# Attention and a gated feed-forward layer on one core: weight rows and weight columns regrouped by four, beta loaded in place

## The chip, the cores and the metric

The kernel runs on one core of a Trainium2 chip. The core has five engines that run side by side and wait for one another by semaphores: PE (TensorE, matrix products), DVE (VectorE), ACT (ScalarE), POOL (GpSimd) and SP (SyncE, which here only issues transfers). PEld is the weight loading of PE, a row of its own in the profile. Transfers (DMA) are issued by SP, ACT or POOL and carried by 16 DMA engines. The metric is the device time of one execution in microseconds (us); lower is better.

## The reference

The reference computes causal attention for 4 batches of 8 heads, 768 positions and 64 values a head, and sends the result through a feed-forward layer. Heads 0, 2 and 6 see all earlier positions; the others see the first 4 positions and a window of 64.

```python
scores = q @ k.T / sqrt(64)                 # per batch and head, masked as above
a      = softmax(scores)
x      = (a @ v) laid out as [3072 tokens, 512]
h      = x @ w_in                           # [3072, 2048]
g      = h * (1 / (1 + exp(-beta * h)))     # beta has one value for each of the 2048 columns of h
out    = g @ w_out                          # [3072, 512]
```

The columns of h, the values of beta and the rows of w_out share one index, d_ff (0 to 2047). The sum in the last line runs over it, so that it may be walked in any order, if it is the same order for all three.

## The kernel before

The work is cut into 8 chunks (4 batches, 2 halves of 384 positions) and 32 units (a chunk and a pair of heads). A unit is loaded, transposed, multiplied to scores (`sp`, lines L422 and L451, PE), sent through the exponential (`es`, L460, ACT), masked (L478 and following, DVE) and multiplied with the values (`po`, L520, PE), normalized on DVE and transposed to `xT`. A chunk of `xT` then passes the feed-forward layer in two parts:

- Part one (`steps_G1`) goes by 16 groups `fi` of 128 columns of h. A group has 4 products over d_model (L588, each with a weight load of 128x128 from `w_in_sb` and 384 tokens passing), a tanh on ACT with beta as scale (`th`, L593), and a gate on DVE (`gT`, L596).
- Part two (`steps_G2`) sums over the 16 groups for 128 tokens at a time: 16 products (L641, L626 for the last tokens) with `gT` as weights and `w_out_sb[:, fi, :]` passing; ACT copies the sum out (`osb`) and SP stores it.

Both weight matrices stay in SBUF in bf16. Each is loaded by 4 POOL transfers, which also convert from float32: `load_w_in` (L140) takes a quarter of w_in's columns (512 of them, all four blocks of 128 rows); `load_w_out` (L144) takes 512 rows of w_out. Beta is loaded at the start by ACT as 16 rows of 128, transposed by PE (`beta_go`, L671) and halved on DVE into `beta_h` (L672).

The order of the instructions on each engine is written out by hand and kept: `RAMP` is a list of words for the first 8 units, `PLAN` and `TAIL` for the rest. In `RAMP`, `lq` and `lv` are loads of q, k and v on SP; `wi0` to `wi3` and `wo0` to `wo3` the weight loads on POOL; `ck`, `cq`, `cv` casts; `tk`, `tq` transposes on PE and `kk`, `kq` their copies; `ma` masks on DVE; `be` beta; `hm` and `hf` the first and the second half of a group of part one, `mm` and `mA` a whole group, `mb` a piece of part two. Every engine works its list strictly in order. What an instruction waits for (semaphores of other engines and of transfers) is derived from the tiles that it reads and writes. The transfers of SP and ACT share 8 semaphores in turn, so that each of them waits for the one issued 8 before it; POOL's transfers have 8 of their own (`DMASW0` to `DMASW7`), and the weight loads are the first eight of these.

Of the kernel before, what the change touches and what calls it, by code (L numbers as in the profile page):

```python
# [10 lines left out]
F32 = mybir.dt.float32  # L11
BF16 = mybir.dt.bfloat16
ALU = mybir.AluOpType
# [5 lines left out]
def kernel(  # L19
# [13 lines left out]
    nc = tc.nc  # L33
# [4 lines left out]
    FO = d_ff // 128  # L38
    HALF = S // 2
# [16 lines left out]
    stage = ctx.enter_context(tc.tile_pool(name="stage", bufs=2))  # L56
# [5 lines left out]
    ps_m = ctx.enter_context(tc.tile_pool(name="ps_m", bufs=3, space=bass.MemoryType.PSUM))  # L62
# [10 lines left out]
    def later(delay, fn):  # L73

        todo = [fn]

        def once():
            if todo:
                todo.pop()()
        heapq.heappush(heap, (clock[0] + delay, count[0], once))  # L80
        count[0] += 1
        return once

    def flush(upto):
        while heap and heap[0][0] <= upto:
            heapq.heappop(heap)[2]()

    def step(s):
        cost, fn = s
        flush(clock[0])  # L90
        clock[0] += cost
        fn()
# [4 lines left out]
    xT = {}  # L97
# [36 lines left out]
    w_in_sb = wpool.tile([128, MO, d_ff], BF16, name="w_in_sb")  # L134
    w_out_sb = wpool.tile([128, FO, d_model], BF16, name="w_out_sb")
    beta_h = wpool.tile([128, FO], F32, name="beta_h")
# [4 lines left out]

    def load_w_out(i):
        f = slice(i * 4, (i + 1) * 4)
        nc.gpsimd.dma_start(out=w_out_sb[:, f, :], in_=moe_w_out.rearrange("(fo fi) d -> fi fo d", fi=128)[:, f, :])  # L144
        w_done.add(i)

    load_qk(0, 0, 2)
# [1 line left out]
    warm = consts.tile([1, 1], F32, name="warm")  # L149
    nc.vector.memset(warm, 0.0)  # L150
    nc.scalar.activation(out=warm, in_=warm, func=ACTF.Exp)
    br = stage.tile([FO, 128], F32, name="beta_r", bufs=1)
    nc.scalar.dma_start(out=br, in_=moe_beta.rearrange("(fo fi) -> fo fi", fi=128))


    zeros = consts.tile([128, 512], BF16, name="zeros")
# [1 line left out]
    ident_f = consts.tile([128, 128], F32, name="idf")  # L158
# [81 lines left out]
    def cast(u, name, copy):  # L240
        b, h2, p = units[u]
        c = u // NPAIR
        s = st_u.setdefault(u, {})
        if "qkb" not in s:
            s["qkb"] = att.tile([128, 2, HT, 2, D], BF16, name="qkb", bufs=4)
        copy(out=s["qkb"][:, "qk".index(name)], in_=staged[name, c, p // 2][:, p % 2:4:2].rearrange("p h t d -> p t h d"))
# [328 lines left out]
    def spare_bank():  # L575
        return ps_s.tile([128, 2, 512], F32, name="sp")[:, 0]
# [3 lines left out]
    def steps_G1(c):  # L580
        def begin(fi):
            if c not in gTs:
                gTs[c] = moe.tile([128, FO, HALF], BF16, name="gT")
            return spare_bank() if wide[0] else ps_m.tile([128, 512], F32, name="mm")

        def product(fi, hp, some):
            for mo in some:
                nc.tensor.matmul(hp[:, 0:HALF], w_in_sb[:, mo, fi * 128:(fi + 1) * 128], xT[c][:, mo, :],  # L588
                                 start=(mo == 0), stop=(mo == MO - 1))

        def end(fi, hp):
            th = moe.tile([128, HALF], F32, name="th", bufs=3)
            nc.scalar.activation(out=th, in_=hp[:, 0:HALF], func=ACTF.Tanh, scale=beta_h[:, fi:fi + 1])  # L593

            def gate():
                nc.vector.scalar_tensor_tensor(out=gTs[c][:, fi, :], in0=th, scalar=1.0, in1=hp[:, 0:HALF],  # L596
                                               op0=ALU.add, op1=ALU.mult)
            gates.setdefault(c, []).append(later(700, gate))

        def grp(fi, some=range(MO)):  # L600

            def go():
                if 0 in some:
                    partial[c, fi] = begin(fi)
                product(fi, partial[c, fi], some)
                if MO - 1 in some:
                    end(fi, partial.pop((c, fi)))
            return (len(some) * 163, go)
        halves[c] = lambda fi, i: grp(fi, range(i * MO // 2, (i + 1) * MO // 2))
        return [grp(fi) for fi in range(FO)]  # L610
# [55 lines left out]
    due = [max(i for i, x in enumerate(first) if x[0] == c) + 1 for c in range(NCHUNK)]  # L666
    done = [0, 0]

    def beta_go():
        bp = ps_m.tile([128, 512], F32, name="mm")  # L670
        nc.tensor.transpose(bp[:, 0:FO], br, ident_f[0:FO, 0:FO])  # L671
        nc.vector.tensor_scalar(out=beta_h, in0=bp[:, 0:FO], scalar1=0.5, scalar2=None, op0=ALU.mult)  # L672

    def run(steps):
        for x in steps:
            step(x)
# [8 lines left out]
    def do(word):  # L685

        what, n, i, eng = re.fullmatch(r"([a-z]{2}|[a-z][A-Z])(\d*)\.?(\d*)([vag]?)", word).groups()
        n, i = int(n or 0), int(i or 0)
        if what in ("ck", "cq"):
            cast(n, what[1], copies[eng])  # L690
        elif what in ("tk", "tq"):
            step((170, lambda: transpose_qk(n, what[1])))
        elif what in ("kk", "kq"):
            copy_qk(n, what[1], copies[eng])
        elif what == "ko":
            sinks_of(n)
        elif what in ("ad", "qk", "ex", "ma"):
            if n not in visits:
                visits[n] = steps_QK(n)
            step((0 if what in ("ex", "ma") else 170, lambda: visits[n][what](i)))  # L700
        elif what == "cv":
            cast_v(n, i, copies[eng])
        elif what == "vo":
            sink_values(n)
        elif what == "pv":
            pv = products.setdefault(n, [])
            if not pv:
                pv.extend(steps_PV(n))
            run(pv[:2])
            del pv[:2]  # L710
        elif what == "no":
            normalize(n)
        elif what == "xd":
            x_by_dma(n)
        elif what == "xx":
            run(steps_X(n))
        elif what == "cx":
            copy_x(n, copies[eng])
        elif what == "on":
            ones_v(engines[eng], n)  # L720
        elif what == "ne":
            negatives([(0, 1, 2), (3, 4)][n])
        elif what == "be":
            step((100, beta_go))
        elif what == "lv":
            load_v(n, held=eng == "g", tiles=[i])
        elif what == "lq":
            load_qk(n, i, held=eng == "g")
        elif what == "wi":
            load_w_in(n)  # L730
        elif what == "wo":
            load_w_out(n)
        elif what == "rq":
            rows_queries()
        elif what == "rk":
            rows_keys()
        elif what == "ro":
            if n not in more_rows:
                more_rows[n] = load_rows(n)
            more_rows[n].pop(0)()  # L740
        elif what in ("dk", "dq"):
            transposes_dma(n, what[1])
        elif what == "ml":
            late[n].pop(0)()
        elif what == "tt":
            run(steps_T(n))
        elif what == "hm":
            opened.append(done[0])
            done[0] += 1
            step(halves[0](opened[-1], 0))  # L750
        elif what == "hf":
            step(halves[0](opened.pop(0), 1))
        else:
            feed({"mm": "a", "mA": "A", "mb": "b"}[what])

    def feed(x):
# [12 lines left out]
            wide[0] = False  # L769

    RAMP = """
        on0g ck0a lv0.0g cq0g lv0.1 ne0 ck2a tq0 ck1v cq1g lv0.2 lq1.0g kq0a be tk0 ne1 kk0v tq1
        ad0.0 qk0.0 ad0.1 kq1a tk2 lq1.1g qk0.1 lv1.0 ex0.0 cv0.0g ck3v cv0.1v lv1.1 ad1.0 cq2a cq3g ex0.1 tk1
        tk3 ad1.1 kk1a kk2a pv0 kk3a tq2 ko1 ko2 vo0 qk1.1 qk1.0 cv0.2g kq2a ex1.1 ck4v pv0 wi0
        lv1.2 ad2.0 ex1.0 ad2.1 qk2.0 qk2.1 tq3 pv1 lq2.0 pv0 pv1 pv1 cq4g lv2.0 tq4 ko3 ex2.0 ad3.0
        kq3a ml0 ex2.1 tk4 pv2 no0 qk3.0 ad3.1 ck5g qk3.1 no1 kk4a xx0 ex3.0 ck6v tk6 pv3 cq5g
        kq4v pv2 pv3 ad4.0 pv2 ex3.1 ck7g ad4.1 ad5.0 qk4.1 cq6g lv2.1 no2 cq7g lv2.2 kk6a pv3 cx0a
        tq5 ko6 kq5v tk5 ex4.1 qk4.0 kk5a ad5.1 ko5 tq6 qk5.0 no3 wi1 tq7 tk7 ex4.0 qk5.1 xx1
        ad6.0 kq6v ex5.0 wi2 qk6.0 kk7v wi3 on1v ex5.1 ad6.1 lq2.1g qk6.1 ma5.0 cv1.0g ml1 ko7 rk cv1.1g
        cx1a ex6.0 hm ma5.1 cv1.2g ex6.1 mm lv3.0g mA kq7v vo1 pv4 wo0 hf pv4 lv3.1 ad7.0 pv4  # L780
        wo1 lv3.2 pv5 no4 qk7.0 wo2 ex7.0 ad7.1 wo3 pv5 qk7.1 rq pv5 pv6 hm cq8g no5 pv7
        pv6 ex7.1 pv7 pv7 ml1 hf pv6 xx2 no7 no6 cx2a mA mA xx3 cx3a mm mm mm
        mA ro3 mm mm mm mA ck8a mA mm mm mm ro3 mA ro3 mm mm mA mA
        mm ro3 ro3 mm mm mA mA mm mm mA tt8 mA mb ro3 mb mb mb mb
    """
    words = RAMP.split()
    on_vector = {int(w[2]) for w in words if w.startswith("ma")}
# [33 lines left out]
    for t in range(8, NU + 2):  # L821
        c, i = (t + 5) // NPAIR, (t + 5) % NPAIR
# [3 lines left out]
        c, i = (t + 4) // NPAIR, (t + 4) % NPAIR  # L826
        if t >= 12 and c < NCHUNK and i < HT:
            later(2500, lambda c=c, i=i: load_v(c, tiles=[i]))
        c, i = (t + 3) // NPAIR, (t + 3) % NPAIR
# [30 lines left out]
    i = 0  # L860
# [39 lines left out]
```

## Time and profile before

| | before |
|---|---|
| median of 3 runs (lowest to highest) | 229.83 us (229.36 to 231.32) |
| the profiled execution: time, span | 230.81 us, 228.8 us |
| PE, PEld busy in the span | 218.9 us, 125.3 us |
| ACT, DVE, POOL busy | 156.6, 139.3, 87.7 us |
| part one on PE (L588): 512 products of 384 tokens | 326 ns each in the record |
| part two on PE (L641): 368 products of 512 columns | 379 ns each in the record |
| w_in loads (L140): 4 of 512 KB, issue to landing | 9.3 us median |
| w_out loads (L144): 4 of 512 KB, issue to landing | 16.4 us median |
| beta load: 8 KB, issue to landing | 4.1 us |

The times in the views are microseconds from the start of the span. A matmul's record includes its way through the array, and the next one starts before it ends; how fast PE works shows in the distance of their starts. A line of a view by time names start, length, engine, source line, operation and operands; "x6" says that six instructions were merged, and a bracket at the end gives the idle time of that engine just before and what ended it. In the views a transfer stands with the engine that issues it.

### The profile page before, as it was taken

To read this page: it belongs to the slowest core of one execution; us is meant where nothing else is said; L and a number is where in the kernel's file an instruction comes from. 1 tells how busy PE (TensorE), PEld (TensorE's weight loads), DVE (VectorE), ACT (ScalarE), POOL (GpSimd) and SP (SyncE) were. 2 spreads that over 40 slices of the span, in tenths; PEclk is the share of its full clock that TensorE was granted. 3 is DMA by queue.
4 is the path that set the end of the run, shared out by engine and by line. 5 is a ranking of instruction groups with operands and counts; after the bars stand their busy time and mean duration, and the time that the engine had idled before them with its cause. 6 is when DMAs were issued, how large, how long until landed. Compare 5 with 4: busy or idle time off the path is not lost.

```text
span 228.8 us, 5022 instructions
## 1 busy us (share of the span) xinstructions
PE 218.9 (96%) x1907; PEld 125.3 (55%) x1907; DVE 139.3 (61%) x333; ACT 156.6 (68%) x261; POOL 87.7 (38%) x147
## 2 busy tenths in 40 slices
PE   6679999999999999899999999999999999999993
PEld 2446765554655665546654565456645566456553
DVE  3357788853584879327951697576895488128600
ACT  3869899947767797637962796788866687138521
POOL 6386952158360449920296005980180000000000
PEclk9999999999999999999999999999999999999999
DMA  6999999999999499999699668899673111110012
GB/s 205 233 303 230 229 199 197 197 220 170 171 185 190 95 134 156 141 197 165 162 96 140 159 115 126 123 177 108 132 86 83 47 57 27 49 56 36 0 50 92
DMA packets 95384, 31.67 MB, mean 138 GB/s; under 512 B 81776, under 2 KB 92416, under 8 KB 95360
## 3 DMA queue, kind: packets, MB, share of 16 engines
q1 hardware_dynamic: 58880, 22.82, 50.3%
q0 software_dynamic: 35904, 8.13, 41.6%
q10 hardware_dynamic: 576, 0.40, 0.6%
q8 instruction: 15, 0.25, 0.5%
q14 instruction: 9, 0.07, 0.1%
HBM read 27.27 MB, written 6.29 MB: 147 GB/s over the span
## 4 chain that ended last, share of the span: by engine, by line
PE 89%; DMA 6%; SPq 2%; issue 0%; DVE 0%; ACTq 0%; POOL 0%; ACT 0%; DVEq 0%; POOLq 0%
PE mm L641 34%; PE mm L588 25%; PE sp L588 12%; PE sp L451 6%; PE po L520 6%; DMA s<-in_q_dram 4%; DMA QTD<-s 2%; PE mm L626 2%; PE mm L322 1%; SPq L132 1%; PE sp L422 1%; PE mm L558 1%; PE mm L451 1%; PE mm L520 1%; SPq L119 0%
## 5 line engine op out<-in xcount | busy, mean ns | idle before, releaser
L641 PE MATMUL mm<-w_out_sb,gT 128*128 128x512 bf16 x368 | 86.4, 379 | 0.0
L460 ACT ACTIVATE es<-sp 128x768 bf16<-128x768 f32 (+2 forms) x72 | 56.7, 844 | 14.3 <-PE sp L451 14.2
L588 PEld LDWEIGHTS <-w_in_sb 128*128 128x128 bf16 x512 | 47.6, 98 | 29.5 <-issue 0.2
L588 PE MATMUL mm<-xT,w_in_sb 128*128 128x384 bf16 x344 | 63.6, 326 | 0.0
L593 ACT ACTIVATE th<-mm,beta_h 128x384 f32<-128x384 f32 x86 | 49.0, 589 | 6.6 <-PE mm L588 2.3
L596 DVE SCALAR_TENSOR_TENSOR gT<-th,mm 128x384 bf16<-128x384 f32 x86 | 46.2, 552 | 9.6 <-ACT th L593 5.9
L641 PEld LDWEIGHTS <-gT 128*128 128x128 bf16 x368 | 33.0, 98 | 34.4 <-issue 0.9
L282 POOL DMA_DIRECT2D s<-in_q_dram x30 | 22.4, 771 | 43.1 <-DMA QTD<-s 37.5
L645 ACT ACTIVATE osb<-mm 128x512 f32<-128x512 f32 x23 | 13.8, 601 | 32.1 <-PE mm L641 31.2
L588 PE MATMUL sp<-xT,w_in_sb 128*128 128x384 bf16 x168 | 33.0, 326 | 0.0
L520 PEld LDWEIGHTS <-es 128*128 128x128 bf16 x472 | 24.1, 98 | 13.9 <-issue 1.7
L520 PE MATMUL po<-VX,es 128*128 128x65 bf16 x360 | 26.6, 194 | 0.5 <-POOL VX L251 0.5
L593 ACT ACTIVATE th<-sp,beta_h 128x384 f32<-128x384 f32 x42 | 24.4, 585 | 3.1 <-PE sp L588 0.7
L596 DVE SCALAR_TENSOR_TENSOR gT<-th,sp 128x384 bf16<-128x384 f32 x42 | 22.9, 552 | 5.1 <-ACT th L593 3.2
L282 POOL DMA_DIRECT2D s<-in_k_dram x30 | 22.3, 754 | 8.1 <-DMA w_out_sb<-in_moe_w_out_dram 5.2
L478 DVE TENSOR_TENSOR es<-es,Mh 128x768 bf16<-128x768 bf16 (+1 forms) x26 | 17.0, 679 | 13.1 <-ACT es L460 12.5
L451 PE MATMUL sp<-QTD,KT 64*128 64x128 bf16 (+2 forms) x258 | 18.9, 240 | 0.8 <-DMA QTD<-s 0.6
L251 POOL CAST VX<-vs 128x512 bf16<-128x512 f32 x17 | 10.9, 649 | 20.0 <-DMA vs<-in_v_dram 20.0
L529 DVE RECIPROCAL rec<-po 128x6 f32<-128x6 f32 x28 | 5.3, 191 | 18.8 <-PE po L520 18.8
L533 DVE TENSOR_TENSOR x<-po,rec 128x384 bf16<-128x384 f32 x28 | 15.6, 558 | 1.0
L451 PEld LDWEIGHTS <-KT 64*128 64x128 bf16 x278 | 11.2, 94 | 6.9 <-issue 5.1
L259 POOL COPY VO<-VX 128x512 bf16<-128x512 bf16 x16 | 9.6, 622 | 5.1 <-DVE VX L251 5.1
(71 smaller groups left out, 156.4 us busy)
## 6 DMA issues: line engine op xcount, KB each, us to landing
vs<-in_v_dram SPq DMA_DIRECT2D x24, 256.0 KB, 5.8
out_dram<-osb SPq DMA_DIRECT2D x23, 256.0 KB, 2.9
w_in_sb<-in_moe_w_in_dram POOLq DMA_DIRECT2D x4, 512.0 KB, 9.3
w_out_sb<-in_moe_w_out_dram POOLq DMA_DIRECT2D x4, 512.0 KB, 16.4
s<-in_k_dram POOLq DMA_DIRECT2D x30, 64.0 KB, 4.5
s<-in_q_dram POOLq DMA_DIRECT2D x30, 64.0 KB, 4.6
s<-in_k_dram SPq DMA_DIRECT2D x4, 384.0 KB, 6.8
s<-in_q_dram SPq DMA_DIRECT2D x4, 384.0 KB, 8.7
```

The lines of the kernel that those rows point to most:

```text
L251: copy(out=VX[b % 2][:, h2 * HT + t, :, 0:D], in_=staged["v", c][:, t])
L282: nc.gpsimd.dma_start(out=ROWS[c % 2, name][:, t, i * 4 * D:(i + 1) * 4 * D].rearrange("p (h d) -> p h d", d=D), in_=src[b, i:H:2, r:r + 1 ...
L451: nc.tensor.matmul(sps[i][r][:, x * 128:y * 128], key(a, lhs), s["QT"][half(a), qi * 128:(qi + y - x) * 128], start=first, stop=first or y ...
L460: nc.scalar.activation(out=views[i].rearrange("p r k j -> p r (k j)"), in_=banks[2][:, :, 0:n * 128], func=ACTF.Exp, scale=scale)
L478: nc.vector.tensor_mul(ev[:, :, 0:n], ev[:, :, 0:n], Mh[h2][:, None, m0:m0 + n].to_broadcast([128, 2, n, 128]))
L520: nc.tensor.matmul(po[:, qi, hh, :], e, val, start=(j == 0), stop=(j == len(lst) - 1))
L533: nc.vector.tensor_mul(xg[g][:, :, :, u % 2, :].rearrange("p a t d -> p t a d"), po[:, :, :, 0:D], rec.to_broadcast([128, HT, 2, D]))
L588: nc.tensor.matmul(hp[:, 0:HALF], w_in_sb[:, mo, fi * 128:(fi + 1) * 128], xT[c][:, mo, :], start=(mo == 0), stop=(mo == MO - 1))
L593: nc.scalar.activation(out=th, in_=hp[:, 0:HALF], func=ACTF.Tanh, scale=beta_h[:, fi:fi + 1])
L596: nc.vector.scalar_tensor_tensor(out=gTs[c][:, fi, :], in0=th, scalar=1.0, in1=hp[:, 0:HALF], op0=ALU.add, op1=ALU.mult)
L641: nc.tensor.matmul(op, gTs[c][:, fi, ns * 128:(ns + 1) * 128], w_out_sb[:, fi, :], start=(fi == 0), stop=(fi == FO - 1))
L645: nc.scalar.activation(out=osb, in_=op, func=ACTF.Copy, scale=0.5)
```

## The change

The index d_ff is walked in another order. Before, group `fi` held the columns 128 fi to 128 fi + 127. Now the groups go by four: within a block q of 512, group 4q + f holds the columns 512 q + 4 p + f for p = 0 to 127. With that a partition p needs four rows of w_out that lie next to each other in memory (8 KB in float32), which one descriptor fetches, where four pieces of 2 KB were needed. The products of part one read their weights from `w_in_sb` with a step of four columns; w_in itself is loaded as before. Beta is loaded in that order straight to its 128 partitions, in pieces of four values, so that the transpose falls away; the load moves from ACT, at the start, to SP, behind the v loads of the second chunk (new word `lb`), and the halving on DVE (word `be`) moves to just ahead of the first `hm`. `beta_go` no longer counts as a step of 100 in the planner's clock. Lines after the beta load have numbers one lower than before, up to the new function (L588 becomes L587).

```diff
     def load_w_out(i):
         f = slice(i * 4, (i + 1) * 4)
-        nc.gpsimd.dma_start(out=w_out_sb[:, f, :], in_=moe_w_out.rearrange("(fo fi) d -> fi fo d", fi=128)[:, f, :])
+        nc.gpsimd.dma_start(out=w_out_sb[:, f, :], in_=moe_w_out.rearrange("(q fi f) d -> fi q f d", fi=128, f=4)[:, i])
...
-    br = stage.tile([FO, 128], F32, name="beta_r", bufs=1)
-    nc.scalar.dma_start(out=br, in_=moe_beta.rearrange("(fo fi) -> fo fi", fi=128))
+    br = stage.tile([128, FO], F32, name="beta_r", bufs=1)
...
-                nc.tensor.matmul(hp[:, 0:HALF], w_in_sb[:, mo, fi * 128:(fi + 1) * 128], xT[c][:, mo, :],
+                nc.tensor.matmul(hp[:, 0:HALF], w_in_sb[:, mo, fi // 4 * 512 + fi % 4:(fi // 4 + 1) * 512:4], xT[c][:, mo, :],
                                  start=(mo == 0), stop=(mo == MO - 1))
...
+    def load_beta():
+        nc.sync.dma_start(out=br.rearrange("p (q f) -> p q f", f=4), in_=moe_beta.rearrange("(q fi f) -> fi q f", fi=128, f=4))
+
     def beta_go():
-        bp = ps_m.tile([128, 512], F32, name="mm")
-        nc.tensor.transpose(bp[:, 0:FO], br, ident_f[0:FO, 0:FO])
-        nc.vector.tensor_scalar(out=beta_h, in0=bp[:, 0:FO], scalar1=0.5, scalar2=None, op0=ALU.mult)
+        nc.vector.tensor_scalar(out=beta_h, in0=br, scalar1=0.5, scalar2=None, op0=ALU.mult)
...
         elif what == "be":
-            step((100, beta_go))
+            beta_go()
+        elif what == "lb":
+            load_beta()
```

In the words of `RAMP`:

```diff
-        ... lq1.0g kq0a be tk0 ne1 ...
+        ... lq1.0g kq0a tk0 ne1 ...
-        ... wi0 lv1.2 ad2.0 ...
+        ... wi0 lv1.2 lb ad2.0 ...
-        ... cx1a ex6.0 hm ma5.1 ...
+        ... cx1a ex6.0 be hm ma5.1 ...
```

More of the change, by code (lines that the diff above doesn't have):

```diff
@@ L771 @@
     RAMP = """
[L772 to L775, printed above, removed]
+        on0g ck0a lv0.0g cq0g lv0.1 ne0 ck2a tq0 ck1v cq1g lv0.2 lq1.0g kq0a tk0 ne1 kk0v tq1 ad0.0
+        qk0.0 ad0.1 kq1a tk2 lq1.1g qk0.1 lv1.0 ex0.0 cv0.0g ck3v cv0.1v lv1.1 ad1.0 cq2a cq3g ex0.1 tk1 tk3
+        ad1.1 kk1a kk2a pv0 kk3a tq2 ko1 ko2 vo0 qk1.1 qk1.0 cv0.2g kq2a ex1.1 ck4v pv0 wi0 lv1.2
+        lb ad2.0 ex1.0 ad2.1 qk2.0 qk2.1 tq3 pv1 lq2.0 pv0 pv1 pv1 cq4g lv2.0 tq4 ko3 ex2.0 ad3.0
         kq3a ml0 ex2.1 tk4 pv2 no0 qk3.0 ad3.1 ck5g qk3.1 no1 kk4a xx0 ex3.0 ck6v tk6 pv3 cq5g
@@ L779 @@
         ad6.0 kq6v ex5.0 wi2 qk6.0 kk7v wi3 on1v ex5.1 ad6.1 lq2.1g qk6.1 ma5.0 cv1.0g ml1 ko7 rk cv1.1g
[L780 to L784, printed above, removed]
+        cx1a ex6.0 be hm ma5.1 cv1.2g ex6.1 mm lv3.0g mA kq7v vo1 pv4 wo0 hf pv4 lv3.1 ad7.0
+        pv4 wo1 lv3.2 pv5 no4 qk7.0 wo2 ex7.0 ad7.1 wo3 pv5 qk7.1 rq pv5 pv6 hm cq8g no5
+        pv7 pv6 ex7.1 pv7 pv7 ml1 hf pv6 xx2 no7 no6 cx2a mA mA xx3 cx3a mm mm
+        mm mA ro3 mm mm mm mA ck8a mA mm mm mm ro3 mA ro3 mm mm mA
+        mA mm ro3 ro3 mm mm mA mA mm mm mA tt8 mA mb ro3 mb mb mb
+        mb
     """
```

## The prediction

> **What bounds the kernel now.** I read four views in this order: busy time by engine, the chain that ended last, the order in time of TensorE, and the order in time of GpSimd with the landings of its loads.
>
> ```profile
> PE 218.9 (96%) x1907; PEld 125.3 (55%) x1907; DVE 139.3 (61%) x333; ACT 156.6 (68%) x261; POOL 87.7 (38%) x147
> ...
> PE 89%; DMA 6%; SPq 2%; issue 0%; DVE 0%; ACTq 0%; POOL 0%; ACT 0%; DVEq 0%; POOLq 0%
> ```
>
> TensorE (PE) is busy 96% of the span and holds 89% of the last chain. Where the missing 10 us lie shows in a table by stretches (PE, PEld, DVE, ACT, POOL busy, then clock, DMA share, GB/s):
>
> ```profile
> 23.00:35.30 12.30, 12.30 (x124) 8.19 (x123) 9.70 (x23) 10.93 (x19) 8.68 (x15) 1.00 1.20 213
> 35.30:47.00 11.70, 11.70 (x78) 7.18 (x76) 9.71 (x18) 10.66 (x21) 2.96 (x4) 1.00 1.22 195
> 47.00:60.00 13.00, 13.00 (x90) 6.12 (x89) 6.01 (x16) 8.31 (x16) 8.94 (x12) 1.00 1.61 202
> 60.00:90.00 30.00, 29.96 (x317) 18.22 (x316) 22.22 (x60) 23.54 (x39) 13.60 (x19) 1.00 1.42 149
> 90.00:96.00 6.00, 5.40 (x68) 3.17 (x66) 3.02 (x8) 3.04 (x5) 5.94 (x10) 1.00 1.65 142
> 96.00:150.00 54.00, 53.99 (x445) 29.58 (x444) 32.96 (x85) 36.51 (x61) 23.44 (x35) 1.00 1.00 141
> 150.00:222.00 72.00, 71.98 (x555) 39.99 (x552) 44.01 (x94) 46.05 (x76) 9.65 (x13) 1.00 0.44 70
> ```
>
> From 23 to 222 us PE is idle for 0.66 us in all, 0.60 of it in one place near 95 us. So from 23 us on nothing that another engine or a transfer gets earlier can shorten the kernel, and whatever stops PE is added in full. The order in time around 23 us, PE first, then POOL:
>
> ```profile
> 22.85 1.15 PE L588 MATMUL mm<-xT,w_in_sb 128*128 128x384 bf16 x6
> 23.84 0.81 PE L588 MATMUL sp<-xT,w_in_sb 128*128 128x384 bf16 x4
> ...
> 13.35 0.88 POOL L140 DMA_DIRECT2D w_in_sb<-in_moe_w_in_dram  x1
> 20.50 2.22 POOL L140 DMA_DIRECT2D w_in_sb<-in_moe_w_in_dram  x3
> 35.52 0.74 POOL L282 DMA_DIRECT2D s<-in_k_dram  x1 [1.79 <-DMA w_in_sb<-in_moe_w_in_dram]
> ```
>
> The first product with w_in starts at 22.85. Only the first quarter of w_in is there by then: issued at 13.35, it took 8.4 us to land (21.8). The other three were issued between 20.5 and 22.7, just ahead. The line's own view, for the last one (issued at 22.0):
>
> ```profile
> DMA to landing us min/median/max: 13.3/13.3/13.3
> ```
>
> So the fourth quarter lands at 22.0 + 13.3 = 35.3 us, and a POOL load that waits for the same semaphore starts at 35.52. PE runs through 23 to 35 without a gap because each product waits for its own quarter alone, and the later quarters are wanted later.
>
> **The change part by part.** *The strided weight columns.* The old group fi reads 128 adjacent columns, inside one quarter; the new group reads every fourth column of the same quarter, so the data it needs is the same. What it waits for is not. The instruction lists of the two kernels as built differ here (row, line, instruction, wait), before first:
>
> ```
> 400 L588 Ldweights w_in_sb [waits DMASW0_49]
> 402 L588 Ldweights w_in_sb
> ...
> 399 L587 Ldweights w_in_sb [waits DMASW0_49]
> 401 L587 Ldweights w_in_sb [waits DMASW3_49,DMASW2_49,DMASW1_49]
> ```
>
> DMASW0 to 3 are the four w_in loads. Before, the waits for 1, 2 and 3 stand at rows 554, 662 and 694, hundreds of instructions later; now all three stand at the second weight load of the first group. Step and blocks together seem to be taken as one interval that crosses all four loads. PE works its list in order, so everything behind row 401 waits too: the po products of attention, the scores, ACT's tanh, DVE's gates. PE would issue row 401 at about 23.0 and gets it at 35.3: **12.3 us**. Nothing in the diff moves the three issues at 20.5 to 22.7: POOL's list is the same up to there. Bounds: from the 35.52 on, POOL starts a load each time the next w_out load lands, at 35.52, 38.86, 42.25 and 45.58, so a load takes about 3.35 us; the earliest landing is 20.5 + 7.2 (the shortest issue to landing of the line) + 2 x 3.35 = 34.4. The latest: beta's packets, below, 1.0 us more, 36.3. Stall 11.4 to 13.3 us.
>
> *PE's restart.* The longest PE idle in this trace after the first matmul is 1.0 us, so the price of a 12 us stop has no row. The nearest is the beginning, where PE comes from rest: eight matmuls of 512 columns (L167) from 1.29 take 3.59 us, the last one 0.63 of it, that is (3.59 - 0.63) / 7 = 0.42 us each; in L641 at the end 32 of them take 7.07 us, 0.22 each. The eight cost some 8 x 0.2 = **1.7 us** more than later. I take this once; bounds 0 (no slow stretch) and 3.4 (twice as long). The clock column says 1.00 there too, so I go by the spacing.
> [...]
>
> *The width of the strided loads.* 512 weight loads of L588 (98 ns each in the groups) run beside matmuls that follow each other every 0.65 / 4 = 162 ns (four from 23.84, the next group 0.65 later). What a contiguous load really occupies shows in L520: 26 pairs of weight load and 65-column matmul take 0.95 us, the last record 0.19, so a pair takes 30 ns. A step of 8 bytes could make that four times as long, 120 ns, and is still covered by 162. I take 0; lower bound 0, upper in the rivals.
>
> *w_out by 8 KB rows.* 4 x 512 pieces become 4 x 128. The bytes stay; four POOL instructions of 756 ns get shorter at most. Before, the w_out loads landed from about 38 to 48 us and PE's first product with them was at 47.2; with PE 14 us later this has slack. 0.
>
> *beta.* Gone are an ACT issue (416 ns, while ACT loads its table), a 201 ns matmul that PE waited 0.7 us for (6.16), and a DVE instruction of 175 ns. But the chain up to 14.8 us is a row of SP issues and the landing of a q load (9.55, 5.26 us to landing), on which PE waits again; the 0.7 falls into that. Moving beta also shifts the eight shared semaphores by one, so that SP's loads wait for a transfer one earlier; SP is issuing without a break from 4.75 to 9.4, so that yields nothing. 0, bounds 0 to -0.3.
> Added are one SP issue behind the v loads (about 17 us) with 512 pieces of 16 bytes. The mean packet of that queue took 50.3% x 16 x 228.8 / 58880 = 31 ns, so 512 of them are 1.0 us of all 16 engines at most, by which SP's later loads (L119, L132) slide; their users stand behind row 401. And a DVE instruction that now waits for beta, just ahead of a mask and a QTD copy that ran at 22.6 and 22.9. SP's loads of that time land 7.6 to 10.9 us after issue, so beta lands at 25 to 28 and DVE stands for 2 to 5 us. This is hidden under PE's stop until 35.3; without the stop PE's products behind those masks would wait as long.
>
> *The gap near 95 us.* PE waits 0.60 us there for a QTD transpose. POOL's row loads no longer wait for w_out once PE is 14 us later, so half may go: -0.3, bounds 0 and -0.6.
>
> **Sum.** 12.3 + 1.7 + 0 + 0 + 0 - 0.3 = +13.7 us. The profiled execution took 230.81 (span 228.8 and 2.0 around it), which gives 244.5. It lies 1.0 above the median of the three runs, 229.83; for the median I say **243.5**. Lowest terms: 11.4 + 0 - 0.6 - 0.3 = +10.5, that is 240.3. Highest: 13.3 + 3.4 = +16.7, that is 246.5.
>
> **The rivals.** *The wait does not bite (not slower).* If the three loads had landed before PE came to row 401, or the wait fell away, PE would run on and the change would be worth beta alone: 229.5 to 229.8. It decides at 23.0 us, the landing of the last quarter against that. For it: groups 0 to 3 need nothing of the other quarters. Against it: the built list, and landings of 7.2 to 13.3 us after issues at 20.5 to 22.0. 4%.
> *Strided loads bound PE as well.* From 162 ns on, a load sets the pace of all 512. Were it eight times the contiguous 30 ns, 240 ns, that adds 512 x 78 ns = 40 us: 283. For it: no row has a stepped weight read. Against it: 130 ns are free per load. 6%.
> *Beta lands last.* The v loads around 22 us took 21.6 us to land; at that pace beta would come at 17 + 21.6 = 38.6, DVE would hold the masks, and the stop would end 3.3 us later, 246.8. Against it: beta has 512 short packets and goes ahead of those loads. 5%.
>
> **How the numbers follow.** The forecast has 85%. The range takes in the bounds of landing and restart, and a little for how single runs lie (229.36 to 231.32): 239.5 to 247.5; it leaves out the first two rivals, 10%, and a tail of the forecast. A measurement of this kernel can tell about 1%, 2.3 us, from no change. Faster by more than that has no mechanism here: 1%. Within 1% is the first rival: 4%. Slower: 95%.
>
> **What would show it.** Right: one PE gap of about 12 us from 23 us, ended by the w_in load, at the second weight load of L587; matmul spacing doubled for some 3 to 4 us after it; then no idle; all later stages moved by about 14 us; L587 at 162 ns a matmul. Wrong: PE running through 23 to 35 us, spacing above 162 ns in the products with w_in, or PE waiting for beta_h or masks after the w_in loads have landed.

## The result, and the profile after

| | before | changed |
|---|---|---|
| median of 4 runs (lowest to highest) | 230.57 us (229.36 to 231.56) | 243.41 us (242.98 to 244.76) |
| the profiled execution: time, span | 230.81, 228.8 us | 242.98, 240.9 us |

The changed kernel takes 1.0569 times as long (95% interval 1.0494 to 1.0645). The forecast was 243.5. Ratios, here and below, leave out executions over 1.5% longer than the fastest of the same kernel; medians and ranges hold all of them.

On the page of the changed kernel, PE's share has fallen although it does the same work (the row of busy tenths, one digit for each 6 us, has a hole in its fifth and sixth slice, and the granted clock is low in the fifth to seventh), and one group of products has an idle time before it that names its releaser:

```profile
PE 219.9 (91%) x1887; PEld 133.7 (55%) x1906; DVE 138.2 (57%) x333; ACT 156.6 (65%) x261; POOL 87.9 (36%) x147
...
PE   7786039999999999999999999999999999999993
...
PEclk9999558999999999999999999999999999999999
...
L587 PE MATMUL mm<-xT,w_in_sb 128*128 128x384 bf16 x344 | 64.9, 330 | 11.9 <-DMA w_in_sb<-in_moe_w_in_dram 11.8
L587 PEld LDWEIGHTS <-w_in_sb 128*128 128x128 bf16 x512 | 55.5, 114 | 35.9 <-issue 13.7
```

(PE's count is 20 lower than before; one of them is beta's transpose, and the other 19 are records missing from the trace, since PEld has only one less, beta's.) In order of time on PE, the first product with w_in runs alone, and the second comes 12 us later:

```profile
21.77 0.35 PE L587 MATMUL mm<-xT,w_in_sb 128*128 128x384 bf16 x1
33.96 1.76 PE L587 MATMUL mm<-xT,w_in_sb 128*128 128x384 bf16 x5 [11.84 <-DMA w_in_sb<-in_moe_w_in_dram]
35.52 1.49 PE L587 MATMUL sp<-xT,w_in_sb 128*128 128x384 bf16 x4
```

The three later w_in loads were issued earlier than before (19.42, before 20.50), and so both ends of the stop came earlier:

```profile
19.42 2.23 POOL L140 DMA_DIRECT2D w_in_sb<-in_moe_w_in_dram  x3
```

The four products from 35.52 are spread over 1.49 us; before, the same four took 0.81. What the clock did is in the table by stretches (PE, PEld, DVE, ACT, POOL busy, then granted clock, DMA share, GB/s):

```profile
21.80:34.00 12.20, 0.36 (x4) 0.15 (x3) 1.30 (x3) 1.34 (x2) 5.41 (x11) 0.58 1.17 220
34.00:37.50 3.50, 3.50 (x13) 1.70 (x14) 0.56 (x1) 1.04 (x2) 0.00 (x0) 0.50 1.08 225
37.50:41.00 3.50, 3.50 (x64) 2.71 (x63) 3.08 (x9) 2.28 (x5) 2.02 (x4) 1.00 1.07 211
```

During the stop the other engines fall quiet too: DVE works 1.30 and ACT 1.34 of 12.2 us, POOL 5.41. PE then gets half the clock for another 3.5 us and the whole clock from 37.5 on. After that it has no idle gap worth naming until the end; the gap near 95 us of before is gone. In the sum, PE to PE: the second product would have come at 21.77 + 0.16 = 21.93 and came at 33.96, +12.03; half clock from 33.96 to 37.5 loses half of 3.54, +1.77; the gap near 95 us, -0.60; PE reached w_in 1.08 us earlier (21.77, before 22.85), -1.08. That is +12.1, and the span grew by 240.9 - 228.8 = 12.1.

The other moved pieces, each from the order in time of its engine:

```profile
15.94 2.94 SPq L669 DMA_DIRECT2D beta_r<-in_moe_beta_dram  x1
18.98 2.73 SPq L119 DMA_DIRECT2D s<-in_k_dram  x1
...
23.51 0.51 DVE L672 TENSOR_SCALAR beta_h<-beta_r 128x16 f32<-128x16 f32 x1 [1.82 <-DMA beta_r<-in_moe_beta_dram]
```

The issue of beta's load held SP for 2.9 us, and DVE stood for 1.8 us until beta was there. PE has no wait that ends with either: its stop runs from 22.1 to 33.96 us, when beta is long there.

### The profile page after: what moved, and what is told of

Same layout as the page of the kernel before. It is cut to its first block, busy times and chain, and to the rows that moved or that the text cites. A ratio compares the mean times of both kernels' runs of the same rounds, so it can differ in the third digit from the quotient of the medians.

```text
span 240.9 us, 5001 instructions
## 1 busy us (share of the span) xinstructions
PE 219.9 (91%) x1887; PEld 133.7 (55%) x1906; DVE 138.2 (57%) x333; ACT 156.6 (65%) x261; POOL 87.9 (36%) x147
## 4 chain that ended last, share of the span: by engine, by line
PE 78%; DMA 9%; DVE 3%; ACT 3%; POOL 2%; issue 2%; SPq 1%; POOLq 0%; ACTq 0%
PE mm L640 30%; PE mm L587 22%; PE sp L587 11%; DMA w_in_sb<-in_moe_w_in_dram 5%; PE po L519 5%; PE sp L450 5%; DMA s<-in_q_dram 2%; DMA xT<-x 2%; PE mm L625 1%; DVE gT L595 1%; ACT es L459 1%; SPq L132 1%; PE mm L321 1%; PE mm L450 1%; DVE x L532 1%
## 5 line engine op out<-in xcount | busy, mean ns | idle before, releaser
L640 PE MATMUL mm<-w_out_sb,gT 128*128 128x512 bf16 x349 | 83.5, 379 | 1.1 <-issue 0.2
L587 PE MATMUL mm<-xT,w_in_sb 128*128 128x384 bf16 x344 | 64.9, 330 | 11.9 <-DMA w_in_sb<-in_moe_w_in_dram 11.8
L587 PEld LDWEIGHTS <-w_in_sb 128*128 128x128 bf16 x512 | 55.5, 114 | 35.9 <-issue 13.7
L595 DVE SCALAR_TENSOR_TENSOR gT<-th,mm 128x384 bf16<-128x384 f32 x86 | 46.3, 552 | 19.9 <-ACT th L592 16.4
L587 PE MATMUL sp<-xT,w_in_sb 128*128 128x384 bf16 x168 | 33.6, 331 | 0.2
L519 PEld LDWEIGHTS <-es 128*128 128x128 bf16 x472 | 24.3, 98 | 13.5 <-issue 2.0
L519 PE MATMUL po<-VX,es 128*128 128x65 bf16 x360 | 26.7, 194 | 0.2 <-POOL VX L250 0.2
L595 DVE SCALAR_TENSOR_TENSOR gT<-th,sp 128x384 bf16<-128x384 f32 x42 | 22.9, 552 | 5.8 <-ACT th L592 3.9
L477 DVE TENSOR_TENSOR es<-es,Mh 128x768 bf16<-128x768 bf16 (+1 forms) x26 | 15.3, 617 | 13.1 <-ACT es L459 12.5
L250 POOL CAST VX<-vs 128x512 bf16<-128x512 f32 x17 | 11.5, 680 | 20.0 <-DMA vs<-in_v_dram 7.8
L258 POOL COPY VO<-VX 128x512 bf16<-128x512 bf16 x16 | 10.1, 650 | 23.1 <-DVE VX L250 23.1
```

What stands on the lines that cost most here:

```text
L250: copy(out=VX[b % 2][:, h2 * HT + t, :, 0:D], in_=staged["v", c][:, t])
L477: nc.vector.tensor_mul(ev[:, :, 0:n], ev[:, :, 0:n], Mh[h2][:, None, m0:m0 + n].to_broadcast([128, 2, n, 128]))
L519: nc.tensor.matmul(po[:, qi, hh, :], e, val, start=(j == 0), stop=(j == len(lst) - 1))
L587: nc.tensor.matmul(hp[:, 0:HALF], w_in_sb[:, mo, fi // 4 * 512 + fi % 4:(fi // 4 + 1) * 512:4], xT[c][:, mo, :], start=(mo == 0), stop=(mo ...
L640: nc.tensor.matmul(op, gTs[c][:, fi, ns * 128:(ns + 1) * 128], w_out_sb[:, fi, :], start=(fi == 0), stop=(fi == FO - 1))
```

## The experiments

Each ran beside the kernel before on its chip; in the first four its median was 230.55 us (23 runs), in the others 230.96 us (29 runs). The theory was that the stop is a wait which the stepped read of one large tile brings with it, and nothing else of the change matters; the main rival, that the stepped reads or the small pieces cost something themselves.

### w_in in four tiles, the rest of the change kept

```diff
-    w_in_sb = wpool.tile([128, MO, d_ff], BF16, name="w_in_sb")
+    w_in_sb = [wpool.tile([128, MO, 512], BF16, name=f"w_in_sb{i}") for i in range(4)]
...
-... w_in_sb[:, mo, fi // 4 * 512 + fi % 4:(fi // 4 + 1) * 512:4] ...
+... w_in_sb[fi // 4][:, mo, fi % 4:512:4] ...
```

> The changed kernel with w_in in four tiles, one for each load, so that a stepped read touches one tile only; steps of four columns, 8 KB rows of w_out and the new way of beta are all kept. Theory (the stop is the wait for all four loads, and the steps cost nothing): no PE gap at 22 us, the weight loads stay at about 113 ns but hidden, time about 1.0 us under before for PE's earlier start (21.8 instead of 22.9), of which the late beta may take 0.2: 229.7 against a before of 230.6. Rival (the stepped reads themselves cost something on PE): the products with w_in stay over 162 ns each and the time stays above 232.

Measured: 230.97 us median of 12, ratio 1.0015 (0.9981 to 1.0049). PE in order of time, with two later lines that have a gap before them:

```profile
21.86 1.17 PE L587 MATMUL mm<-xT,w_in_sb 128*128 128x384 bf16 x6
22.86 0.81 PE L587 MATMUL sp<-xT,w_in_sb 128*128 128x384 bf16 x4
...
25.71 0.38 PE L421 MATMUL sp<-Ns,idb 128*128 128x256 bf16 x2 [0.45 <-DVE gT L595]
...
95.24 0.51 PE L450 MATMUL sp<-QTD,KT 64*128 64x384 bf16 x8 [0.75 <-DMA QTD<-s]
```

The stop is gone, the four products take 0.81 us again, and with them the whole loss: each quarter is waited for when it is wanted. The weight loads have the median of 113 ns here too, so their width is not the cause. The gain of 1 us that I had expected did not come. PE did reach w_in at 21.86, but lost 0.45 us behind DVE, whose work stood behind the late beta, and 0.75 us near 95 us; the median is no lower than before.

### The wait alone

The kernel before, adjacent columns, with PE made to touch all four quarters first:

```diff
+    def touch():
+        nothing = ps_m.tile([128, 512], F32, name="mm")
+        for i in range(4):
+            nc.tensor.matmul(nothing[:, 0:128], w_in_sb[:, 0, i * 512:i * 512 + 128], zeros[:, 0:128], start=True, stop=True)
...
-        cx1a ex6.0 hm ma5.1 ...
+        cx1a ex6.0 xw hm ma5.1 ...        # xw calls touch()
```

> The kernel before, with four small matmuls of 128 columns put ahead of the first product with w_in, one from each quarter of w_in, their output never read; nothing else is changed, columns adjacent, w_out and beta as before. Theory (the wait alone makes the loss): a PE gap of about 12 us from 22.9 to 35.3, half clock after it for some 3.5 us, no gap near 95 us: +12.3 +1.75 -0.8 = +13.3, some 243.8. Rival (steps or pieces make a share of it): less than +10.

Measured: 245.01 us median of 4 (244.72 to 245.66), ratio 1.0623 (1.0561 to 1.0684). PE in order of time, then its stretches:

```profile
22.81 0.23 PE L677 MATMUL mm<-zeros,w_in_sb 128*128 128x128 bf16 x1 [0.46 <-DMA w_in_sb<-in_moe_w_in_dram]
28.87 0.29 PE L677 MATMUL mm<-zeros,w_in_sb 128*128 128x128 bf16 x1 [5.82 <-DMA w_in_sb<-in_moe_w_in_dram]
32.28 0.29 PE L677 MATMUL mm<-zeros,w_in_sb 128*128 128x128 bf16 x1 [3.13 <-DMA w_in_sb<-in_moe_w_in_dram]
35.59 0.29 PE L677 MATMUL mm<-zeros,w_in_sb 128*128 128x128 bf16 x1 [3.02 <-DMA w_in_sb<-in_moe_w_in_dram]
```

```profile
26.00:35.60 9.60, 0.59 (x3) 0.23 (x4) 0.00 (x0) 0.00 (x0) 5.34 (x8) 0.53 1.21 196
35.60:40.00 4.40, 4.40 (x20) 2.36 (x21) 0.83 (x2) 1.30 (x3) 1.48 (x2) 0.50 1.23 199
40.00:44.00 4.00, 4.00 (x64) 2.91 (x62) 3.36 (x11) 2.61 (x5) 0.74 (x1) 0.96 1.20 193
```

The wait alone makes a loss as large as that of the change (the two intervals overlap), on a kernel with neither steps nor large pieces nor the new beta. The four touches let one see the landings one after another: each small matmul starts as its quarter lands. The half clock lasted longer here: from 35.6 until a little after 40 us (the last stretch has 0.96 of the clock), 4.7 us and so 2.3 us lost, where the changed kernel lost 1.8.

### PE kept at work through the wait

```diff
+    def busy(n):
+        nothing = ps_m.tile([128, 512], F32, name="mm")
+        for i in range(n):
+            nc.tensor.matmul(nothing, zeros[:, 0:128], zeros, start=True, stop=True)
...
-        cx1a ex6.0 be hm ma5.1 ...
+        cx1a ex6.0 be xi48 hm ma5.1 ...   # xi48 calls busy(48)
```

> The changed kernel with 48 matmuls of 512 zero columns on PE ahead of the first product with w_in, their output never read; they take 48 x 0.216 = 10.4 of the 11.8 us that PE stands there. Theory (after the stop PE runs at half clock for 3.6 us and loses 1.75): PE idle only for about 1.5 us, granted clock 1.00 throughout, first products with w_in at 162 ns, time 243.4 - 1.75 = 241.7. Rival (the slow products after the stop come from the stepped weights or from a crowd of waiting work, not from the idling): 243.4.

Measured: four executions of 241.85, 243.46, 246.34 and 246.57 us, ratio 1.0519 (1.0440 to 1.0598), which rests on the first two. This interval overlaps that of the changed kernel, so the time does not decide. The profiled execution (241.85 us) does show the mechanism, in order of time and by a stretch:

```profile
21.69 10.53 PE L677 MATMUL mm<-zeros 128*128 128x512 bf16 x48
32.06 0.33 PE L587 MATMUL mm<-xT,w_in_sb 128*128 128x384 bf16 x1
33.61 0.97 PE L587 MATMUL mm<-xT,w_in_sb 128*128 128x384 bf16 x5 [1.22 <-DMA w_in_sb<-in_moe_w_in_dram]
34.42 0.81 PE L587 MATMUL sp<-xT,w_in_sb 128*128 128x384 bf16 x4
```

```profile
33.60:38.00 4.40, 4.39 (x59) 3.21 (x60) 2.60 (x7) 2.96 (x5) 0.00 (x0) 1.00 1.07 218
```

Five products take 0.97 us where they took 1.76 after the idle stop, at the whole clock, with the same stepped weights and the same work piled up. So the slow products come with PE's idling: 0.50 of the clock after the idle stop, 1.00 here. What they cost in the median is not settled by this kernel; its profiled execution also waited 1.27 us for a QTD transpose at 105 us, which the changed kernel did not.

### Beta alone

The beta part on the kernel before: the load on SP behind the v loads, `be` ahead of `hm`, no transpose (the diff of the change, without its lines for w_out and w_in).

> The kernel before with the beta part of the change alone (columns of w_in and rows of w_out in the old order, so that beta's values meet the wrong columns; the work is the same). Theory (PE's earlier start in the changed kernel, 21.8 instead of 22.9, comes from the beta part): PE reaches the first product with w_in at about 21.8; 1.0 us under before, less up to 0.2 for the masks that wait for beta on DVE: 229.7 against 230.6. Rival (the earlier start lies between executions, or with other parts): 230.6.

Measured: 230.44 us median of 12, ratio 1.0000 (0.9969 to 1.0032). The time did not fall by the 1.0 us of the theory. In the profiled execution PE reached w_in at 22.69, but this does not speak against an earlier start. That execution has a stretch at half clock ahead of w_in, which among the other profiled executions only that of the kernel with small pieces of w_out (below) has. The rows of the two:

```profile
12.00:16.00 4.00, 3.68 (x41) 2.81 (x40) 2.28 (x7) 2.28 (x4) 3.50 (x8) 0.57 1.14 316
12.00:16.00 4.00, 3.68 (x41) 2.68 (x39) 2.19 (x6) 2.38 (x4) 3.65 (x8) 0.57 1.14 315
```

Just ahead of it PE, here with beta's part alone, was 0.58 us ahead of the kernel before at the same product (the first line is of before):

```profile
12.91 0.27 PE L422 MATMUL sp<-Ns,idb 128*128 128x256 bf16 x1 [0.32 <-ACT es L460]
...
12.33 0.27 PE L421 MATMUL sp<-Ns,idb 128*128 128x256 bf16 x1 [0.32 <-ACT es L459]
```

The four-tile kernel, with the same way of beta and the whole clock, has this product at 12.21 and reached w_in at 21.86: from 0.12 us the distance grows to 0.83. So in this one execution most of the earlier start was spent in the half clock. That the start is earlier is seen in profiled executions alone; no median shows it.

### Beta's old load kept as well, unread

The four-tile kernel, with the old load by ACT at the start into a tile of its own:

```diff
+    br_old = stage.tile([FO, 128], F32, name="beta_o", bufs=1)
+    nc.scalar.dma_start(out=br_old, in_=moe_beta.rearrange("(fo fi) -> fo fi", fi=128))
```

> The kernel with w_in in four tiles, and in addition the old load of beta (16 rows of 128) by ACT at the start, into a tile that nobody reads; PE does not wait for it. Theory (the early SP loads go sooner in the changed kernel because beta's load no longer takes a turn of the eight semaphores): the last of the first q loads is issued at 4.2 us again, not 3.35, and the first k load of the second chunk at 8.2 to 8.4, not 7.4 to 7.8; time up by some 0.5, within the spread. Rival (PE's wait for the transposed beta, or DVE's instruction, made the difference): SP's issues stay at 3.35 and about 7.6.

Measured: 231.14 us median of 10, ratio 1.0020 (0.9985 to 1.0055). SP in order of time:

```profile
4.12 0.37 SPq L119 DMA_DIRECT2D s<-in_q_dram  x1
4.77 2.75 SPq L132 DMA_DIRECT2D vs<-in_v_dram  x3
7.62 1.18 SPq L119 DMA_DIRECT2D s<-in_k_dram  x1
```

Half of the expectation holds: the last of the first q loads waits for its turn again (4.12). But the k load goes at 7.62 all the same, so that the turn does not reach PE. The first 22 us took 21.7 to 22.9 us in the profiled executions of the different kernels. The half clock shown above is a part of it where it occurs; the rest is left open, and no median shows it.

### Beta by POOL, early

The four-tile kernel; `load_beta` issues on POOL, and `lb` stands behind `lq1.1g` in `RAMP`.

> The kernel with w_in in four tiles, but beta's load issued by POOL behind the loads of the second chunk's q and k (about 6 us, where POOL has nothing to do until 9) instead of by SP behind the v loads at 16 us. Theory (in the four-tile kernel the earlier start is spent again because beta lands at 23.4 and DVE holds the masks): beta lands by 12 us, SP's issue of 2.8 us is gone, no PE gap at 25 us; 0.6 us under the four-tile kernel, 230.4 by its median, a little under before. Rival (late beta costs nothing, the difference lies between executions): 231.0 as the four-tile kernel.

Measured: 231.31 us median of 12, ratio 1.0034 (1.0000 to 1.0068). Beta landed at 10.8 us (5.8 and 5.0 to landing), DVE no longer waited for it and PE's gap at 25 us was gone; yet the time did not fall. The profiled execution has gaps elsewhere, 0.55 us until 71.06 (for a QTD transpose) and 1.41 us until 144.97 (for DVE), where other kernels have theirs at 95 or 105. The rival holds: half a microsecond at 25 us is lost in what lies between executions.

### w_out in small pieces

The four-tile kernel, with w_out loaded as four transfers of 2 KB pieces, one f each, over all blocks q.

> The kernel with w_in in four tiles, but w_out in pieces of 2 KB as before (each of the four transfers takes one row of four from all partitions and blocks, so that the order of d_ff is kept). Theory (the size of the pieces of w_out lies on no path): 231.0 as the four-tile kernel; POOL's four issues take about 755 ns again, not 550, and the last w_out load lands a few us later, still ahead of its first use. Rival (8 KB pieces gain or lose something in the stage from 25 to 60 us): a difference of over 1 us.

Measured: 230.72 us median of 10, ratio 0.9980 (0.9942 to 1.0018). The theory holds: the loads landed 16.4 us after their issue in the median, as before, where the 8 KB pieces took 14.5 in the four-tile kernel. POOL waited 9.2 us for the small pieces; for the large ones it did not wait in the four-tile kernel, and 7.7 us in the two kernels with beta by POOL and with the unread load. PE waited for neither.

### Steps of sixteen columns

```diff
-... w_in_sb[:, mo, fi // 4 * 512 + fi % 4:(fi // 4 + 1) * 512:4] ...
+... w_in_sb[:, mo, fi:d_ff:FO] ...
-... moe_w_out.rearrange("(q fi f) d -> fi q f d", fi=128, f=4)[:, i] ...
+... moe_w_out.rearrange("(fi f) d -> fi f d", f=FO)[:, f] ...
```

> The changed kernel with steps of sixteen columns (32 bytes) instead of four (8 bytes): group fi takes the columns 16 p + fi, w_out lies sixteen rows to a partition (its four loads still take four of them each, 8 KB), beta is loaded in pieces of 64 bytes. The first product waits for all four loads of w_in, as in the changed kernel. Theory (weight loads are wide of the 162 ns of a product): they take longer than 113 ns in the record, but the products stay at 162 ns each, time 243.4. [...]

Measured: 245.84 and 247.64 us, ratio 1.0669 (1.0587 to 1.0750). What its view of w_in's tile shows (duration in ns, least, median, greatest):

```profile
L587 PEld LDWEIGHTS <-w_in_sb x512: 141/145/183, 35.7 to 231.2; 128*128 128x128 bf16 x171
L587 PE MATMUL mm<-xT,w_in_sb x344: 323/326/527, 35.7 to 230.7; 128*128 128x384 bf16 x172
```

The weight loads widen from 98 ns (adjacent) over 113 (steps of 4) to 145 (steps of 16), and where these products follow each other they stay at 163 ns from start to start (162 before). There the theory holds. It does not hold behind the short products of attention (65 columns, L519), as the same four products show in the four-tile kernel and then here:

```profile
130.58 0.81 PE L587 MATMUL mm<-xT,w_in_sb 128*128 128x384 bf16 x4
131.23 0.22 PE L519 MATMUL po<-VX,es 128*128 128x65 bf16 x2
...
147.11 0.85 PE L587 MATMUL mm<-xT,w_in_sb 128*128 128x384 bf16 x4
147.80 0.22 PE L519 MATMUL po<-VX,es 128*128 128x65 bf16 x2
```

The four take 0.69 us instead of 0.65. There are 30 places of this kind; the second product comes some 31 ns later than before at each, 0.9 us in all, and with steps of four 2 ns later. The time was missed by 3 us. Besides this, the last quarter of w_in landed later in the profiled execution, so that PE started at 35.74 instead of 33.96 and stood at half clock until 41.1, and PE waited another 1.1 us until 119.17 for the transposed `xT`.
Why the record of a weight load grows with the step was not tested.

## Why the prediction was right, and where its terms were off

- **The stop: right.** Forecast 12.3 us at the second weight load, ended by the last w_in load; measured 12.03, in this place, by this releaser. The tile split took it away and the touching of all quarters made it on the kernel before, so cause and size are both shown. One premise did not hold: I took the three issues as fixed at 20.5 us, and they came at 19.42, as PE came 1.08 earlier; the length came out because both ends moved together. That the three waits come from an interval taken too wide is argued from the lists of instructions; shown is that they go with the one large tile. The interval in question is rather that of the loads than that of the read: the stepped read of one block of rows stays within 512 columns of one quarter, while each load writes four blocks that lie 2048 columns apart. This also fits that the first product, from the first block, waits for its own quarter alone. It is argued, not shown.
- **The restart: right in size.** Forecast 1.7 from PE's first eight matmuls, bounds 0 and 3.4; 1.8 in the changed kernel, 2.3 with the wait alone, and 2.7 with steps of sixteen (5.4 us at half clock). I set the clock column aside because it reads 1.00 at the start; the trace of before has no record of the clock ahead of 4.9 us, and a stretch without a record is shown as 1.00. After the stop the column reads 0.50, and 1.00 again 3.5 us after work resumed in the changed kernel, 4.7 with the wait alone and 5.4 with steps of sixteen. The clock did not fall as soon as PE stood: in the changed kernel it fell at 23.9 us, 1.8 us after PE's last product, and PE had been busy for 2.25 of the 4.0 us ahead of that. Nor does a long stop stand ahead of every fall: ahead of the early half clock from 12.6 to 16.0 us (the kernel with beta alone) PE had been busy for 1.40 of the 2 us from 10 to 12 us, and stood for 0.32 us until 12.33. What sets the moments at which the clock falls and comes back was not shown.
- **The gap near 95 us: forecast at half its size.** Forecast -0.3, and all 0.6 went. In the four-tile kernel, which has no stop, it is there again (0.75). My reason, that POOL's row loads no longer wait for w_out, is not borne out: in the four-tile kernel POOL does not wait for w_out either, and with the wait alone it waits 10.8 us for it while a gap of 0.43 us is left at 110. Why the gap went is open.
- **Beta's part: the step "0, bounds 0 to -0.3" failed in the profiled execution**, where PE reached w_in 1.08 us earlier. The median did not show such a gain when beta's part was alone (1.0000, 0.9969 to 1.0032), though PE was 0.58 us ahead there too until the clock fell. My reason, that SP issues without a break, was incomplete: the third v load alone took 2.1 us to issue before and 1.5 us after, so SP's pace itself varies. Its cause is open.
- **The price of beta's pieces: sought in the wrong place.** I counted 512 packets of 31 ns on 16 engines, 1.0 us; in the trace these packets take 9 ns each, but SP was held for 2.9 us by the issue, and the next load went at 18.98 instead of 17.08. The number of pieces does not explain it: with 128 pieces, in the kernel with steps of sixteen, the issue held SP for 2.4 us. It cost nothing here.
- **Beta's landing:** forecast 25 to 28 us, DVE standing for 2 to 5; measured 23.5 and 1.8. The rival in which beta lands last fell with it.
- **Strided loads: right for steps of four.** 113 ns are covered by 162; behind short products they cost some 2 ns at each of 30 places, where steps of sixteen cost 31.
- **Why 243.5 met 243.41:** I added 13.7 us, in effect, to a median of 229.83. The profiled executions grew by 12.2 and the medians by 243.41 - 230.57 = 12.8, so the sum was 0.9 to 1.5 too large, and the median of before, now of four runs, is 0.7 higher than the one that I started from. The mechanism and its two large terms were right; the closeness of the total is partly luck.

## What to carry to other kernels

Here a change of access pattern changed the waits (12.03 us more) and not the pace of the products that follow each other (162 ns): after such an edit, read the list of instructions for what the first read of each tile waits for, and where that stands in the engine's order. A tile that several transfers fill is best cut into one tile for each transfer, if readers want the parts at different times (here 230.97 us with four tiles, 243.41 with one). On an engine without idle time, price a stop as its length plus the slow start behind it (12.03 and 1.8 us here).

## What the runs showed of the hardware that was not expected

- Beta's load carries 8 KB, and its issue held SP for 2.1 to 2.9 us with 512 pieces of 16 bytes and for 2.4 us with 128 pieces of 64 bytes, near 16 us; on POOL, near 6 us, 512 pieces took 0.89 us. A v load of 1024 pieces of 256 bytes, 256 KB, was issued in 0.4 to 2.3 us ahead of beta's, and behind it in up to 11.4 us (the changed kernel). So the number and size of the pieces do not set the time of an issue on SP by themselves; what does was not tested.
- The clock fell for 3.4 us in the early stage too (0.57 of the clock from 12 to 16 us in the kernels with beta alone and with small pieces of w_out); in the first of the two PE had been busy for 1.40 of the 2 us from 10 to 12 us, in 19 products. In these profiled executions PE reached w_in 0.8 to 0.9 us later than in the four-tile kernel; that it costs time in the end is not shown: executions of the kernel with beta alone with a mean clock of 0.990 and of 1.000 took 229.47 and 231.32 us.
- Pieces of 8 KB instead of 2 KB shortened POOL's issue of a w_out load from 756 to 560 ns, and its landing from 16.4 to 14.5 us in the median (the four-tile kernel with small and with large pieces).
